# A linear-attention and MLP-mixer kernel: batch 0's u made transposed in PSUM, tokens kept in even and odd halves, other weight pieces, a new order

## The chip, the cores and the metric

The kernel runs on one core of one Trainium2 chip. The time is the device time of one execution in microseconds (us). A core has TensorE (PE; its weight loads are listed apart as PEld), VectorE (DVE), ScalarE (ACT), GpSimd (POOL) and SyncE (SP), and 16 DMA engines that move data between the memory (DRAM) and the on-chip memory (SBUF). PE writes its products to PSUM, which has eight banks of 512 float32 per partition; DVE and ACT read PSUM and write SBUF. SP only issues transfers here, and ACT issues some of the stores.

## The reference

Inputs q, k, v and alpha are (4 batches, 8 heads, 768 tokens, 48 columns), float32. For each batch and head a 48 x 48 state is carried over the tokens:

```
state = alpha[t][:, None] * state + outer(k[t], v[t])
y[t]  = q[t] @ state
```

y, with the heads side by side, is x: (4, 768, 384). A mixer follows, for each batch:

```
h   = relu(x.T @ w_tok1) @ w_tok2        # over tokens: 768 -> 256 -> 768
u   = x + h.T
out = u + relu(u @ w_ch1) @ w_ch2        # over columns: 384 -> 1536 -> 384
```

The output is (4, 768, 384), float32.

## The kernel before, in words

**Attention.** The 768 tokens of a batch are cut into three pieces of 256, so there are twelve pieces n = 0 to 11 (three to a batch). A partition holds two neighbouring tokens ("slots" 0 and 1, even and odd), and one load of 393,216 B brings one of alpha, k, q or v for a piece: `ld_at`, `ld_kt`, `ld_qt`, `ld_vt`. Each piece makes cumulated logarithms of alpha on PE (`cum`), their exponentials (`E`, `IE`), the scaled keys and queries (`kk` and `qq`, tiles pkk and pkq), their transposes, the products of keys and queries (`G`), a causal mask on DVE (`mask`, 1024 columns), the state (`K`, `sa`, `sm`) and two tiles of y that are copied out of PSUM as x (`x0`, `x1`). In pieces 0 to 5 the transposes go over PE (`trk`, `trq`) and an eviction (`evk`, `evq`); in 6 to 11 they are DMA transposes issued by SP (`dk`, `dq`), and the query's is copied once more (`pq`). The eviction of queries (`qev`) writes the two slots of a token pair beside each other, so it writes with a step of two; that of keys (`trwev`) writes runs of 64. Token order inside a tile of 128 rows is therefore the plain one.

**Mixer.** For each batch: t1 (twelve products of 384 columns, from x and w_tok1 into two banks), `ht` (relu to SBUF), t2 (for each of six token tiles two products of 384 columns, out of w_tok2 and ht), `u` (DVE adds x to the bank: tile u, tokens on partitions). c1 needs u transposed (tile ut). In batch 0 (`UP = (0,)`) that is done by PE: `up_0_0` to `up_0_2`, six transposes of 128 x 128 each, and three evictions `ut_0_p`. In batches 1 to 3 it is a DMA transpose on SP for each half of the tokens (`ux`). c1 has twelve column groups mc and two token halves, three products of 384 columns each, and a relu to tile rt on ACT or DVE. c2 sums twelve products for each of six token tiles (in four parts of three), and DVE adds u (`o`, three buffers); the store `st` sends the tile of 128 x 384 to DRAM, from SP's or ACT's queue. The last batch's tile 0 goes in two halves of 192 columns.

**Weights.** Each of 16 weight pieces is loaded by one transfer of 393,216 B and cast to bf16 by ACT, POOL or DVE (`cw`): w_tok1 in two pieces, w_tok2 in two (128 rows each), w_ch1 in six (128 rows by 768 columns), w_ch2 in six (256 rows). c1 of the groups mc below 6 needs w_ch1's pieces 0, 1 and 2, the others need 3, 4 and 5.

**Order.** The program is written out ahead: `ORDER` is a list of operations with a letter for the engine (t PE, s ACT, v DVE, g POOL, y SP), `BUFS` gives each tile its buffer. Every engine goes through its own operations in this order, and waits on semaphores for what it reads and for the buffers that it writes. There are 19 buffers for loads (`in`), four for u, two for ut, three for o, and eight PSUM banks. Entries such as `f8_cumw1` are fillers: products out of a zero tile (line 541 writes it, line 643 multiplies with it) that keep PE running while it waits; the number counts units of 512 columns.

Where a helper does the work, the profile names the helper's line: 643 is `mm` (the products of the attention, and the fillers), 712 the PE transposes of keys and queries, 878 t1, 883 t2, 887 the add of u, 894 the transposes of u, 902 c1, 907 c2, 911 the add of o, 745 and 746 copies and casts on ACT and on the other engines, 770 the mask, 584 loads, 600 to 607 weight loads, 624 the stores, 725 and 729 DMA transposes.

Of the kernel before, what the change touches and what calls it, by code (L numbers as in the profile page):

```python
# [101 lines left out]
UP = (0,)  # L102
# [18 lines left out]
def build(g):  # L121
# [8 lines left out]
    def fillers():  # L130
        for o in list(P.ops):
            nm = o.name
            if "PE" in o.eng and (nm[:4] in ("t1_0", "t2_0", "up_0") or nm.split("_")[-1][-1] in "0123" and nm[:2] not in ("t1", "t2", "up", "c1", "c2") and not nm.endswith("10") and not nm.endswith("11")):
                bank = V("one")
                for z in (1, 2, 3, 4, 6, 8, 12):
                    P.op(f"f{z}_{nm}", {"PE": pe([512] * z)["PE"]}, -100, writes=[bank],
                         emit=lambda e, z=z, bank=bank: g.fill(bank, z))


    def attention(n):  # L140
# [68 lines left out]
        else:  # L209
# [4 lines left out]
                    emit=lambda e: g.trwev(e, tpk, bk, n not in SLOT))  # L214
        if n in QX:
            tqx = V("tpk")
            xq = O("dq", {"SP": (1240.0, 1240.0)}, 9, writes=[tqx], reads=[pkq], preds=qq,
                   emit=lambda e: g.xbar(tqx, pkq), dma=("x", 1400.0, 1180.0, 480.0))
            evq = O("pq", either(dve(1024), act(1024 * 1.35, True), {"POOL": (1100.0, 1140.0)}), 9.5, port=True, writes=[tpq], reads=[tqx], preds=[xq],
                    emit=lambda e: g.qev(e, tpq, g.t(tqx)))  # L220
        else:
            bq = V("one")
            trq = O("trq", pe([128] * 8), 8, writes=[bq], reads=[pkq], preds=qq,
                    emit=lambda e: g.trw(bq, pkq))
            evq = O("evq", either(dve(1024 * 1.065), act(1024 * 1.34)), 9, writes=[tpq], reads=[bq], preds=[trq],
                    emit=lambda e: g.qev(e, tpq, g.bank(bq).bitcast(BF16)))
# [82 lines left out]
    def weight(nm, piece, prio, work=1100.0):  # L309
        raw = V("in")  # L310
        o = P.op(f"ldw_{nm}{piece}", LOADQ[0], prio, writes=[raw],
                 emit=lambda e: g.weight(e, nm, piece, raw, o), dma=("i", work, 1500.0, 650.0))
        wl[(nm, piece)] = P.op(f"cw_{nm}{piece}", either(dve(768, nm != "wc1"), pool_cp(768), act(768, True)), prio + 1,
                               reads=[raw], preds=[o], port=True, emit=lambda e: g.wcast(e, nm, piece, raw))

    def mixer(b):
# [15 lines left out]
        us = []  # L332
        for i in range(NS):
            if i % 3 == 0:
                u = V("u")
            bank = V("one")
            o = P.op(f"t2_{b}_{i}", pe([384] * 2), m0 + (1900 + 330 * i) * sc, writes=[bank],
                     reads=[h for h, _ in hts], preds=[h for _, h in hts] + [wl[("wt2", p)] for p in range(2)],
                     emit=lambda e, i=i, bank=bank: g.tok2(bank, i, [h for h, _ in hts]))
            uo = P.op(f"u_{b}_{i}", dve(384), m0 + (1950 + 330 * i) * sc, writes=[u], reads=[bank, x[i][0]], preds=[o],  # L340
                      emit=lambda e, i=i, bank=bank, u=u: g.uadd(u, i, bank, x[i][0]))
            us.append((u, uo))
        ut = V("ut")
        uts = []
        if b in UP:
            for p in range(3):
                bank = V("one")
                o = P.op(f"up_{b}_{p}", pe([128] * 6), m0 + (3900 + 340 * p) * sc, writes=[bank],
                         reads=list(dict.fromkeys([us[2 * p][0], us[2 * p + 1][0]])),
                         preds=[us[2 * p][1], us[2 * p + 1][1]],  # L350
                         emit=lambda e, p=p, bank=bank: g.utr(bank, [us[2 * p][0], us[2 * p + 1][0]], p))
                uts.append(P.op(f"ut_{b}_{p}", either(dve(768, True), act(768)), m0 + (3950 + 340 * p) * sc, writes=[ut],
                                reads=[bank], preds=[o], emit=lambda e, p=p, bank=bank: g.utev(e, ut, bank, p)))
        else:
            for half in range(2):
                uts.append(P.op(f"ux_{b}_{half}", {"SP": (1240.0, 1240.0)}, m0 + (3900 + 500 * half) * sc, writes=[ut],
                                reads=[us[3 * half][0]], preds=[us[3 * half + i][1] for i in range(3)],
                                emit=lambda e, half=half: g.uxbar(ut, us[3 * half][0], half),
                                dma=("x", 1450.0, 1180.0, 480.0)))
        rts = []  # L360
        for mc in range(NDC):
            rt = V("rt")
            ro = []
            for half in range(2):
                bank = V("one")
                o = P.op(f"c1_{b}_{mc}_{half}", pe([384] * 3), m0 + (4900 + 975 * mc + 487 * half) * sc, writes=[bank],
                         reads=[ut], preds=(uts[0:2 + half] if b in UP else [uts[half]]) + [wl[("wc1", p)] for p in ((0, 1, 2) if mc < 6 else (3, 4, 5))],
# [5 lines left out]
        for i in range(NS):  # L373
            hold = 4000.0 if (i >= NS - 3 and b < B - 1) else 0.0
            cuts = [(0, HD // 2), (HD // 2, HD)] if (b, i) == LAST else [(0, HD)]
            for ci, (ca, cz) in enumerate(cuts):
# [3 lines left out]
                for q4 in range(4):  # L380
                    pp = []
                    for mc in range(3 * q4, 3 * q4 + 3):
# [6 lines left out]
                          reads=[bank, us[i][0]], preds=[prev],  # L389
# [20 lines left out]
ld_at1y ld_at0y ln1s ln0s f8_cumw1t f1_cumw1t cumw1t IE1s cumw0t IE0s ld_vt0y E0s vb0g vs0_0g vs1_0v ld_kt0y kk0v  # L410
f8_trk0t f1_trk0t trk0t E1s ld_qt0y qq0v ka0s kb0s kc0v f1_trq0t trq0t ld_kt1y kk1v K0t evq0s s0_0v ld_vt1y vb1s
f1_trk1t trk1t ld_at2y evk0v ln2s f2_G0_0t G0_0t ld_qt1y ka1g sa1_0v f4_cumw2t cumw2t mask0_0v vs0_1s kb1g kc1g vs1_1s
K1t sm1_0g qq1v sa0_1v sm0_1v G1_0t ld_kt2y IE2s E2s trq1t evq1s ib0t mask1_0v f3_y1_0t y1_0t y0_0t evk1v G0_1t sa1_1v
ld_qt2y x1_0s mask0_1v G1_1t ld_vt2y x0_0s vb2s kk2g trk2t kc2s ldw_wt10y qq2g cw_wt10s f2_ia1t ia1t mask1_1v evk2s
trq2t ld_at3y vs1_2g ldw_wt11y evq2v ib1t y1_1t y0_1t vs0_2g ldw_wt21y sm1_1g P3g K2t sa0_2v sm0_2g x0_1s t1_0_0_0t
f1_G0_2t G0_2t ldw_wt20y G1_2t cw_wt20g t1_0_1_0t mask0_2v x1_1s t1_0_1_1t ld_at4y ld_kt3y t1_0_1_2t lnP3s cum3t
cw_wt11s IE3s ia2t y0_2t x0_2s t1_0_0_1t t1_0_0_2t E3s t1_0_0_3t mask1_2v t1_0_1_3t ib2t y1_2t ldw_wc14y t1_0_1_4t
x1_2s t1_0_0_4t f1_t1_0_1_5t t1_0_1_5t ht_0_1v P4g cw_wt21s t1_0_0_5t ht_0_0s f3_t2_0_0t t2_0_0t t2_0_1t u_0_0v ln13s
r13s ldw_wc13y t2_0_2t u_0_1v t2_0_3t u_0_2v t2_0_5t lnP4s t2_0_4t u_0_3v u_0_5v u_0_4v up_0_0t cw_wc14s cw_wc13s
ldw_wc15y up_0_1t ld_qt3y k0a3g kk3g cum4t trk3t cw_wc15g ut_0_0v up_0_2t ut_0_2v ut_0_1s c1_0_11_0t c1_0_8_0t IE4s  # L420
c1_0_11_1t rt_0_8_0v rt_0_11_0v ldw_wc11y q0r3g qq3g c1_0_9_1t rt_0_9_1v ln14s kb3s c1_0_10_0t cw_wc11s c1_0_9_0t
rt_0_9_0v rt_0_11_1v E4s c1_0_7_0t c1_0_10_1t c1_0_7_1t ldw_wc10y r14s cw_wc10s rt_0_10_1v trq3t evk3s rt_0_7_0v
ldw_wc12y ld_vt3y cw_wc12g c1_0_2_0t c1_0_0_1t ka3g rt_0_7_1s c1_0_8_1t rt_0_10_0v vb3v vs1_3g vs0_3g rt_0_0_1v
rt_0_2_0v evq3s ld_at5y ld_qt4y c1_0_1_1t rt_0_8_1v c1_0_3_0t kc3s K3t P5g c1_0_4_1t rt_0_3_0s rt_0_1_1s q0r4g G0_3t
ld_kt4y qq4g s0_3v ln15s G1_3t sa1_3v c1_0_2_1t rt_0_2_1s mask0_3v lnP5s c1_0_1_0t c1_0_5_1t rt_0_5_1s rt_0_1_0s r15s
mask1_3v ldw_wc21y cw_wc21s k0a4g ldw_wc20y c1_0_6_1t rt_0_6_1v c1_0_4_0t kk4v ldw_wc22y c1_0_5_0t c1_0_0_0t cw_wc22s
rt_0_4_0v rt_0_0_0v cw_wc20g rt_0_4_1s c1_0_6_0t rt_0_6_0v c1_0_3_1t trq4t rt_0_3_1v cum5t trk4t ld_kt5y k0a5g
ldw_wc23y rt_0_5_0s c2_0_3_0t c2_0_5_0t evq4s kb4s evk4v ld_qt5y G1_4t mask1_4v G0_4t ld_vt4y c2_0_0_0t IE5s c2_0_0_1t
ka4g cw_wc23s c2_0_3_1t kc4s sm1_3g E5s mask0_4v ib3t y1_3t ldw_wc24y cw_wc24s c2_0_5_1t vb4g vs1_4s x1_3s ia4t
ldw_wc25y vs0_4g cw_wc25s ld_at6y y0_3t kk5v c2_0_3_2t y0_4t q0r5v trk5t evk5s qq5v K4t c2_0_0_2t sa0_4v c2_0_0_3t P6v  # L430
x0_3s ld_at7y sm0_4g o_0_0v trq5t x0_4s sa1_4v P7g evq5s lnP6s c2_0_5_2t c2_0_5_3t ld_vt5y vb5g c2_0_4_0t c2_0_4_1t
ld_kt7y kc5g G1_5t G0_5t lnP7s o_0_5v ib4t y1_4t vs1_5s mask1_5v t1_1_1_0t t1_1_1_1t sm1_4g x1_4s c2_0_4_2t c2_0_3_3t
vs0_5s ld_at8y t1_1_1_2t st_0_5s K5t mask0_5v sa0_5v sm0_5v cum6t t1_1_0_0t ld_kt6y k0a6g t1_1_0_1t ld_qt6y c2_0_2_0t
# [532 lines left out]
```

## Time and profile before

| | |
|---|---|
| median of three runs | 163.48 us (163.34, 163.48, 164.39) |
| span of the profiled execution | 160.5 us |
| PE busy | 154.6 us, 1563 products |
| DVE, ACT, POOL busy | 114.9, 97.8, 80.8 us |
| DMA | 35.05 MB in 76130 packets, mean 218 GB/s |

The three runs are executions of their own; the profiled execution is known by its span, the time from its first to its last instruction, and the median of the runs is 3.0 us longer than that. Times within the profile count from the span's start. PE's busy time is that of pipelined products whose ends are modelled, so a mean of one product (326 ns at 384 columns) is longer than its share of the stream. A share of the DMA engines is the time that packets took, over sixteen engines; packets can overlap.

### The profile page before, as it was taken

Reading aid. Unit: us, or ns where it says so; the run is one execution under the profiler, and the core shown is the slowest. Engines: PE = TensorE matmul, PEld = TensorE weight load, DVE = VectorE, ACT = ScalarE, POOL = GpSimd, SP = SyncE. Lnnn points to the kernel's source line nnn. Section 1 sums busy time; section 2 is a strip of 40 time slices with the busy share of each in tenths; the row PEclk is TensorE's granted clock in tenths of the full one; section 3 lists DMA queues with packets and bytes.
Section 4 is the critical chain, followed back from the end, with each engine's and each line's share of the span. In section 5 each row is a group of like instructions: output and inputs, shape, how many; then the busy total and the mean of one; then the engine's idle time right before and its main releaser. Section 6 shows DMA issues by size and latency. Waiting matters only on the chain.

```text
span 160.5 us, 3971 instructions
## 1 busy us (share of the span) xinstructions
PE 154.6 (96%) x1563; PEld 97.1 (60%) x1563; DVE 114.9 (72%) x206; ACT 97.8 (61%) x179; POOL 80.8 (50%) x94
## 2 busy tenths in 40 slices
PE   7999989999999999999999999999999999999992
PEld 2545565766667676666667666566567665665661
DVE  6099994979889787989969758795886762464222
ACT  3789999998899955897563583269832203343000
POOL 5205897695973649389778852699523000000000
PEclk9999999999999999999999999999999999999999
DMA  4999999999999999999989999989701235111133
GB/s 122 320 324 317 317 374 311 339 333 306 316 347 324 275 278 272 210 228 319 241 202 298 239 315 204 217 196 134 196 21 62 87 79 169 49 49 53 49 129 116
DMA packets 76130, 35.05 MB, mean 218 GB/s; under 512 B 70352, under 2 KB 74320, under 8 KB 76112
## 3 DMA queue, kind: packets, MB, share of 16 engines
q1 hardware_dynamic: 73808, 31.76, 74.1%
q10 hardware_dynamic: 2304, 3.05, 5.3%
q8 instruction: 12, 0.20, 0.5%
q14 instruction: 6, 0.05, 0.1%
HBM read 25.17 MB, written 4.72 MB: 186 GB/s over the span
## 4 chain that ended last, share of the span: by engine, by line
PE 61%; DMA 12%; DVE 6%; ACT 6%; SPq 6%; POOL 4%; issue 3%; DVEq 0%; POOLq 0%
PE ps L907 22%; PE ps L902 21%; PE ps L643 11%; DMA in<-in_v_dram 6%; SPq L584 6%; DMA out_dram<-o 4%; PE ps L878 3%; PE ps L883 2%; DMA ut<-u 2%; DVE pkk L700 2%; DVE gtm L770 1%; PE ps L712 1%; DVE rt L875 1%; POOL vb L746 1%; POOL pkq L700 1%
## 5 line engine op out<-in xcount | busy, mean ns | idle before, releaser
L907 PE MATMUL ps<-wc,rt 128*128 128x384 bf16 (+1 forms) x300 | 52.4, 319 | 0.0
L902 PE MATMUL ps<-ut,wc 128*128 128x384 bf16 x288 | 50.3, 326 | 0.1
L902 PEld LDWEIGHTS <-wc 128*128 128x128 bf16 x288 | 27.1, 98 | 17.9 <-DMA ut<-u 0.6
L907 PEld LDWEIGHTS <-rt 128*128 128x128 bf16 x300 | 27.8, 98 | 16.0
L873 ACT ACTIVATE rt<-ps 128x384 bf16<-128x384 f32 x47 | 21.4, 492 | 23.6 <-PE ps L902 23.3
L875 DVE TENSOR_SCALAR rt<-ps 128x384 bf16<-128x384 f32 x49 | 25.6, 551 | 9.1 <-PE ps L902 8.9
L770 DVE TENSOR_TENSOR gtm<-ps,mk 128x1024 bf16<-128x1024 f32 x24 | 28.5, 1218 | 3.1 <-PE ps L643 2.8
L911 DVE TENSOR_TENSOR o<-ps,u 128x384 f32<-128x384 f32 (+1 forms) x25 | 13.2, 536 | 12.6 <-PE ps L907 10.1
L700 POOL TENSOR_TENSOR pkk<-in,IE 128x768 bf16<-128x768 f32 x8 | 14.5, 1817 | 3.3 <-DVE ss L844 2.3
L745 ACT CAST x<-ps 128x384 bf16<-128x384 f32 x20 | 9.2, 479 | 11.1 <-PE ps L643 9.5
L887 DVE TENSOR_TENSOR u<-ps,x 128x384 bf16<-128x384 f32 x24 | 12.0, 550 | 3.1 <-PE ps L883 2.5
L746 POOL CAST vb<-in 64x384 bf16<-64x384 f32 (+1 forms) x14 | 8.3, 594 | 10.4 <-DMA in<-in_v_dram 4.7
L692 POOL TENSOR_TENSOR in<-in,in 128x384 f32<-128x384 f32 x8 | 8.0, 1000 | 10.5 <-DVE u L887 3.8
L643 PE MATMUL ps<-rt 128*128 128x512 bf16 (+1 forms) x29 | 12.1, 515 | 1.1 <-DVE rt L541 1.1
L745 ACT CAST vb<-in 64x384 bf16<-64x384 f32 (+1 forms) x18 | 11.4, 634 | 0.8 <-DMA in<-in_v_dram 0.3
L700 POOL TENSOR_TENSOR pkq<-in,E 128x768 bf16<-128x768 f32 x6 | 10.9, 1818 | 0.6 <-DMA tpk<-pkq 0.3
L878 PE MATMUL ps<-x,wt 128*128 128x384 bf16 x48 | 11.0, 325 | 0.0
L844 POOL TENSOR_TENSOR ss<-tmp,E 128x384 bf16<-128x384 f32 x10 | 8.3, 833 | 4.2 <-DVE in L628 3.9
L841 DVE TENSOR_TENSOR tmp<-ps,ss 128x384 f32<-128x384 f32 x16 | 8.8, 552 | 1.8 <-PE ps L643 0.6
L883 PE MATMUL ps<-ht,wt 128*128 128x384 bf16 x48 | 9.1, 326 | 0.0
L643 PE MATMUL ps<-vb,gtm 128*128 128x48 bf16 x192 | 8.2, 183 | 0.2 <-DVE gtm L770 0.2
L643 PE MATMUL ps<-tpq,tpk 48*64 48x128 bf16 (+1 forms) x288 | 7.9, 218 | 0.4 <-POOL tpq L746 0.3
(94 smaller groups left out, 207.6 us busy)
## 6 DMA issues: line engine op xcount, KB each, us to landing
in<-in_alpha_dram SPq DMA_DIRECT2D x12, 384.0 KB, 5.1
in<-in_v_dram SPq DMA_DIRECT2D x12, 384.0 KB, 5.6
in<-in_k_dram SPq DMA_DIRECT2D x12, 384.0 KB, 5.2
in<-in_q_dram SPq DMA_DIRECT2D x12, 384.0 KB, 5.5
in<-in_moe_w_ch_dram SPq DMA_DIRECT2D x12, 384.0 KB, 5.9
out_dram<-o ACTq DMA_DIRECT2D x15, 192.0 KB, 1.8
in<-in_moe_w_tok_dram SPq DMA_DIRECT2D x4, 384.0 KB, 6.0
out_dram<-o SPq DMA_DIRECT2D x8, 192.0 KB, 2.2
```

Of the source, the lines that this page charges most:

```text
L643: return self.pe.matmul(out, lhsT=lhsT, rhs=rhs, start=start, stop=stop, skip_group_check=True)
L700: self.shared(self.eng[e].tensor_tensor(self.t(dst)[:, :, h0:h1, 0:D], self.t(src)[:, h0:h1].rearrange("p h s d -> p s h d"), bass.AP(tens ...
L745: return self.act.copy(d, s)
L770: self.nc.vector.tensor_tensor(self.t(gtm)[:, hf, :, :], self.pair(gp).rearrange("p a (j t) -> p (a j) t", t=128), bass.AP(tensor=m.tensor ...
L873: self.act.activation(d, s, AF.Relu)
L875: self.nc.vector.tensor_scalar_max(d, s, 0.0)
L878: self.pe.matmul(self.bank(bank)[:, 0:HD], lhsT=self.wt1[:, kc, m * 128 : m * 128 + 128], rhs=self.t(x), start=(kc == 0), stop=(kc == NS - 1))
L883: self.pe.matmul(self.bank(bank)[:, 0:HD], lhsT=self.wt2[:, kc, i * 128 : i * 128 + 128], rhs=self.t(hts[kc]), start=(kc == 0), stop=(kc = ...
L887: self.nc.vector.tensor_tensor(self.t(u)[:, i % 3], self.bank(bank)[:, 0:HD], self.t(x), ALU.add)
L902: self.pe.matmul(self.bank(bank)[:, 0:HD], lhsT=self.wc1[:, kc, mc * 128 : mc * 128 + 128], rhs=self.t(ut)[:, 3 * half : 3 * half + 3, kc, ...
L907: self.pe.matmul(self.bank(bank)[:, 0 : cz - ca], lhsT=self.t(rts[mc][0])[:, i * 128 : i * 128 + 128], rhs=self.wc2[:, mc, ca:cz], start=( ...
L911: self.nc.vector.tensor_tensor(self.t(o)[:, ca:cz], self.bank(bank)[:, 0 : cz - ca], self.t(u)[:, i % 3, ca:cz], ALU.add)
```

## The change

**Batch 0's u.** `UP` becomes empty and `UDIR = (0,)` is new. For batch 0 and each token half, three banks (one for each 128 columns j) first take x transposed: `xadd` multiplies three tiles of x with the identity, 128 columns each, into one bank (`xa_0_half_j`, 18 products in all). Then `tok2t` adds the t2 products with the operands exchanged, ht as the stationary one and w_tok2 as the moving one (`tt_0_half_j`, two products of 384 columns), so that the bank holds u transposed. `utev3` evicts it to ut (`ut_0_half_j`, on ACT four times and on DVE twice). The adds u_0_i and the PE transposes up_0_p fall away. Because the o adds need u with tokens on partitions, `unat` transposes ut back by a DMA transpose on SP for each half (`un_0_0`, `un_0_1`).

**Token order.** Inside each tile of 128 rows, the even tokens now come first and the odd ones after them. `qev` and `trwev` become one function, `merged`, that writes runs of 64. The masks are built for this order (tiles of the same size). w_tok1's rows are loaded in that order, each piece by two transfers to 64 partitions, and w_tok2's columns are put in that order by its cast. The store sends row (s, p) of a tile to row 2p + s of out.

**Weight pieces.** w_tok2 is cut by columns (one piece to a token half), w_ch1 by columns (256 to a piece, all 384 rows), so that c1 of group mc needs piece mc // 2 alone, and a token half of t2 one piece of w_tok2.

**Order.** ORDER and BUFS are new throughout. The opening now loads alpha of piece 0 first. Its fillers are f12 and f4 ahead of `cumw0`, f6 ahead of `trk0`, f2 ahead of `K0`, f3 ahead of `G0_0` and f2 ahead of `trk2`: 29 units, where there were 36.

```diff
-UP = (0,)
+UP = ()
+UDIR = (0,)
...
-                    emit=lambda e: g.qev(e, tpq, g.bank(bq).bitcast(BF16)))
+                    emit=lambda e: g.merged(e, tpq, g.bank(bq).bitcast(BF16)))
...
+        if b in UDIR:
+            ut, us, uts = V("ut"), [], []
+            for half in range(2):
+                evs = []
+                for j in range(NM):
+                    bank = V("one")
+                    tx = x[3 * half : 3 * half + 3]
+                    xa = P.op(f"xa_{b}_{half}_{j}", pe([128] * 3), ...
+                    o = P.op(f"tt_{b}_{half}_{j}", pe([384] * 2), ...
+                              preds=[h for _, h in hts] + [xa, wl[("wt2", half)]], ...
+                    evs.append(P.op(f"ut_{b}_{half}_{j}", either(act(384), dve(384)), ...
+                uts.append(evs)
+                u = V("u")
+                un = P.op(f"un_{b}_{half}", {"SP": (1240.0, 1240.0)}, ... reads=[ut], preds=evs, ...
+                us += [(u, un)] * 3
...
-  preds=(uts[0:2 + half] if b in UP else [uts[half]]) + [wl[("wc1", p)] for p in ((0, 1, 2) if mc < 6 else (3, 4, 5))],
+  preds=(uts[half] if b in UDIR else uts[0:2 + half] if b in UP else [uts[half]]) + [wl[("wc1", mc // 2)]],
...
+            w = self.w[0].rearrange("(c p s) m -> s p c m", p=64, s=2)[part]
+            self.gated(dma(t[64 * part : 64 * part + 64].rearrange("p (c m) -> p c m", c=3), w[:, 3 * piece : 3 * piece + 3, :]), op)
...
+            w = self.w[2].rearrange("(c p) m -> p c m", p=128)
+            self.gated(dma(t.rearrange("p (c m) -> p c m", c=3), w[:, :, 256 * piece : 256 * piece + 256]), op)
...
+    def rows(self, d):
+        return d.rearrange("(p s) c -> s p c", s=2)
+
     def store(self, e, o, b, i, ca, cz):
-        self.queue(e).dma_start(self.out[b, i * 128 : (i + 1) * 128, ca:cz], self.t(o)[:, ca:cz])
+        self.queue(e).dma_start(self.rows(self.out[b, i * 128 : (i + 1) * 128, ca:cz]), self.t(o)[:, ca:cz])
...
+    def merged(self, e, d, s):
+        self.copy(e, self.t(d).rearrange("p (g s t) -> p s g t", g=8, s=2), s.rearrange("p (s g t) -> p s g t", s=2, g=8))
...
+    def xadd(self, bank, xs, j):
+        for i, x in enumerate(xs):
+            self.mm(self.bank(bank)[:, i * 128 : i * 128 + 128], self.t(x)[:, j * 128 : j * 128 + 128], self.idn, i == 0, False)
+
+    def tok2t(self, bank, half, j, hts):
+        for kc in range(NDT):
+            self.mm(self.bank(bank)[:, 0:HD], self.t(hts[kc])[:, j * 128 : j * 128 + 128],
+                    self.wt2[:, half, kc, :], False, kc == NDT - 1)
+
+    def utev3(self, e, ut, bank, half, j):
+        self.copy(e, self.t(ut)[:, 3 * half : 3 * half + 3, j, :], self.bank(bank)[:, 0:HD].rearrange("p (i t) -> p i t", i=3))
+
+    def unat(self, u, ut, half):
+        self.nc.sync.dma_start_transpose(self.t(u).rearrange("p i (j c) -> p (i j) c", j=NM),
+                                         self.t(ut)[:, 3 * half : 3 * half + 3].rearrange("p i j t -> p (i j t)"))
```

Of the new ORDER, the stretch around batch 0's mixer, and the end:

```
... x1_2s t1_0_0_4t t1_0_1_5t ht_0_1v ldw_wt21y t1_0_0_5t IE3s kk3g ht_0_0s xa_0_1_1t xa_0_0_2t xa_0_1_0t xa_0_1_2t cw_wt21s
tt_0_0_1t ut_0_0_1s tt_0_0_0t ut_0_0_0s tt_0_0_2t ut_0_0_2v ldw_wc13y cw_wc13g tt_0_1_2t ut_0_1_2s tt_0_1_1t ut_0_1_1v tt_0_1_0t
ut_0_1_0s ka3s trk3t evk3v c1_0_7_0t rt_0_7_0v ldw_wc14y cw_wc14g c1_0_9_0t ...
... o_3_1v st_3_1s rt_3_6_1s st_3_0h1s c2_3_5_0t c2_3_2_2t c2_3_2_3t rt_3_4_1v c2_3_5_1t rt_3_9_1s c2_3_5_2t c2_3_5_3t o_3_5v o_3_2v
st_3_2y st_2_0y st_3_5s c2_3_3_0t c2_3_4_0t c2_3_4_1t c2_3_4_2t c2_3_4_3t o_3_4v st_3_4s c2_3_3_1t c2_3_3_2t c2_3_3_3t o_3_3v
st_3_3y c2_3_0h0_2t c2_3_0h0_3t o_3_0h0v st_3_0h0s
```

More of the change, by code (lines that the diff above doesn't have):

```diff
@@ L310, in weight @@
         raw = V("in")
-        o = P.op(f"ldw_{nm}{piece}", LOADQ[0], prio, writes=[raw],
-                 emit=lambda e: g.weight(e, nm, piece, raw, o), dma=("i", work, 1500.0, 650.0))
+        ls = {}
+        for z in range(2 if nm == "wt1" else 1):
+            ls[z] = P.op(f"ldw_{nm}{piece}{'ab'[z] if nm == 'wt1' else ''}", LOADQ[0], prio, writes=[raw],
+                         emit=lambda e, z=z: g.weight(e, nm, piece, z, raw, ls[z]),
+                         dma=("i", work / (2 if nm == "wt1" else 1), 1500.0, 650.0))
         wl[(nm, piece)] = P.op(f"cw_{nm}{piece}", either(dve(768, nm != "wc1"), pool_cp(768), act(768, True)), prio + 1,
-                               reads=[raw], preds=[o], port=True, emit=lambda e: g.wcast(e, nm, piece, raw))
+                               reads=[raw], preds=list(ls.values()), port=True, emit=lambda e: g.wcast(e, nm, piece, raw))
     def mixer(b):
```

277 lines of the change are left out of this document (135 added, 142 removed), and 22 rows, old and new, of the table BUFS.

## The prediction

> **What bounds the kernel now.** I read the page first, then the busy time of each engine by stretches, then the timelines of the opening and of the end.
>
> ```profile
> span 160.5 us, 3971 instructions
> ...
> PE 154.6 (96%) x1563; PEld 97.1 (60%) x1563; DVE 114.9 (72%) x206; ACT 97.8 (61%) x179; POOL 80.8 (50%) x94
> ...
> q1 hardware_dynamic: 73808, 31.76, 74.1%
> q10 hardware_dynamic: 2304, 3.05, 5.3%
> ...
> L643 PE MATMUL ps<-rt 128*128 128x512 bf16 (+1 forms) x29 | 12.1, 515 | 1.1 <-DVE rt L541 1.1
> ```
>
> PE is busy for 154.6 of 160.5 us, and 12.1 us of that are fillers (L643 out of a zero tile), all in the first 28 us. So PE does about 142.5 us of work, and what can be gained lies ahead of the first channel product (c1, L902); from there PE runs almost without a gap, and anything that stops it costs its whole length. The other number to keep is the DMA's: 74% of sixteen engines on SP's queue. In stretches:
>
> ```profile
> 2.00:28.00 26.00, 24.75 (x274) 13.43 (x273) 19.16 (x36) 21.64 (x34) 14.47 (x21) 1.00 1.10 320
> ...
> 70.00:81.00 11.00, 11.00 (x120) 6.96 (x119) 10.35 (x19) 7.44 (x15) 9.21 (x7) 1.00 1.10 256
> 81.00:94.00 13.00, 13.00 (x190) 8.73 (x188) 9.79 (x15) 7.47 (x17) 11.13 (x12) 1.00 0.96 254
> ...
> 114.00:129.00 15.00, 14.72 (x168) 9.80 (x166) 11.59 (x19) 5.16 (x10) 3.80 (x6) 1.00 0.28 84
> 129.00:133.00 4.00, 4.00 (x27) 2.38 (x25) 2.44 (x6) 0.00 (x0) 0.00 (x0) 1.00 0.52 118
> ...
> 137.00:144.00 7.00, 7.00 (x45) 4.21 (x43) 4.16 (x8) 2.94 (x7) 0.00 (x0) 1.00 0.15 56
> ```
>
> The columns are the stretch, busy time (and count) of PE, PEld, DVE, ACT and POOL, the granted clock, the mean busy share of the 16 DMA engines, and GB/s. The share reads 1.10 while loads arrive (packets of one engine overlap), and stays near 1 up to 94 us: the DMA engines have little to spare until then, and it is hidden only because loads run ahead.
>
> **The opening.** The change makes batch 0's u transposed at once. These rows stand between the last x and c1 now:
>
> ```profile
> 21.30 1.30 DVE L746 COPY tpq<-ps 128x1024 bf16<-128x1024 bf16 x1
> ...
> 27.73 2.28 PE L883 MATMUL ps<-ht,wt 128*128 128x384 bf16 x12
> 29.85 0.83 PE L894 MATMUL ps<-idn,u 128*128 128x128 bf16 x12
> 30.52 0.33 PE L643 MATMUL ps<-la,u 128*128 128x384 bf16 x1
> ...
> 30.81 0.61 PE L712 MATMUL ps<-idn,pkk 128*128 128x128 bf16 x8
> 31.25 0.50 PE L894 MATMUL ps<-idn,u 128*128 128x128 bf16 x6
> 31.76 4.55 PE L902 MATMUL ps<-ut,wc 128*128 128x384 bf16 x27
> ...
> 30.16 0.88 POOL L746 CAST wc<-in 128x768 bf16<-128x768 f32 x1 [0.36 <-DMA in<-in_moe_w_ch_dram]
> ...
> L873 ACT ACTIVATE ht<-ps 128x384 bf16<-128x384 f32 x4 | 1.9, 489 | 2.2 <-PE ps L878 2.2
> ...
> L887 DVE TENSOR_TENSOR u<-ps,x 128x384 bf16<-128x384 f32 x24 | 12.0, 550 | 3.1 <-PE ps L883 2.5 <-issue 0.4
> ...
> L746 DVE COPY tpk<-ps 128x1024 bf16<-128x1024 bf16 x3 | 2.0, 679 | 0.0
> ...
> 133.97 10.72 PE ps L902 x66
> ```
>
> (Timeline rows are start, length; the ht, u and tpk rows are groups, with total and mean in ns; the last is a piece of the chain that ended last.) A 384-column product takes 10.72/66 = 0.162 us of the stream. From the start of t2 to c1 it is 31.76 - 27.73 = 4.03 us: twelve products (1.95), six adds on DVE, 18 transposes, their evictions. After, the twelve products go into banks that already hold x, six evictions follow them closely (four on ACT, two on DVE), and PE does only trk3 (0.44, from 30.81 to 31.25 now) before c1: 1.95 + 0.45 = 2.4, saved 1.6. The 18 products with the identity that add x are as many and as large as the 18 transposes removed, and stand in waits ahead of ht; six adds of 0.55 us leave DVE, four evictions of 0.49 come to ACT, beside PE. The last query eviction goes from a strided write, 1.30, to runs of 64, for which I take the key eviction's 0.68: 0.6 less on the last x. cum4 (30.52 to 30.81, 0.3) now comes behind c1 and is still to be done. Together -1.6 - 0.6 + 0.3 = **-1.9 us**. The weights no longer bind: c1 needed three pieces of w_ch1, the last cast at 30.16 to 31.04, the 22nd load; now it needs one, the 19th, and a load takes 393,216 B / 320 GB/s = 1.23 us, so 3.7 us earlier. Bounds of this term: 0 (the new order waits as long elsewhere) and -3.7 (all that the loads allow). If ACT, at 21.64 of 26 us, runs late with the four evictions, c1 slips by up to 0.5 each. Seven filler units fewer (36 to 29, 0.2 us each) change nothing while they only fill waits. The two new DMA transposes (u back to its plain order) are on SP's queue, ahead of loads of batch 2 and needed only by the o adds; they cost DMA time, counted below. The masks, whose shape doesn't change, are free, as are the setup copies.
>
> **The stores.** This is the part that decides. With tokens in halves, row p of a tile is no longer row p of out; `store` now names the DRAM side as (half, pair, column), 2 x 64 x 384, where it was 128 x 384. The bytes and runs (1,536 B) are the same, so counted by packets it costs nothing. The question is how the rows are dealt to the DMA engines.
>
> ```profile
> L624 ACTq DMA_DIRECT2D out_dram<-o x16: 338/338/390, 56.9 to 157.0; - x16
> L624 SPq DMA_DIRECT2D out_dram<-o x9: 332/530/2601, 66.0 to 157.8; - x9
> ...
> DMA to landing us min/median/max: 1.6/2.0/5.8
> ```
>
> q10 carries ACT's 16 stores alone: 2304 / 16 = 144 packets each, 128 rows and 16 more, one for each engine: a store's outermost count, 128, is dealt in sixteen equal shares. Every load and store of before has 128 outermost on both sides, so no row shows what a 2 gives. Two bounds: sixteen engines as now, or two, half a tile each. The nearest row in form is the present store, but what it shows is a deal by equal shares of the outermost count, which 2 cannot give to sixteen; I take two engines.
>
> [...]
>
> Price of a store: from 137 to 144 us there are two stores and nothing else on the DMA (56 GB/s x 7 us = 2 x 196,608 B): 0.15 x 7 x 16 / 2 = 8.4 us of engine time each; by q10, 0.053 x 160.5 x 16 / 15.5 = 8.8. Over sixteen engines that is 0.53 us, over two **4.3 us**. PE makes one such tile in 12 x 0.162 = 1.95 us when it does nothing else, and there are three o tiles, so DVE's o add waits for the store three back. That wait exists already in small (0.39 and 1.64 us):
>
> ```profile
> 53.51 0.55 DVE L911 TENSOR_TENSOR o<-ps,u 128x384 f32<-128x384 f32 x1
> ...
> 70.02 0.56 DVE L911 TENSOR_TENSOR o<-ps,u 128x384 f32<-128x384 f32 x1 [0.39 <-DMA out_dram<-o]
> 87.04 0.55 DVE L911 TENSOR_TENSOR o<-ps,u 128x384 f32<-128x384 f32 x1
> ...
> 134.74 0.56 DVE L911 TENSOR_TENSOR o<-ps,u 128x384 f32<-128x384 f32 x1 [1.64 <-DMA out_dram<-o]
> ...
> 157.44 0.36 DVE L911 TENSOR_TENSOR o<-ps,u 128x192 f32<-128x192 f32 x1 [0.43 <-PE ps L907]
> ...
> 57.47 1.77 SPq L584 DMA_DIRECT2D in<-in_k_dram  x1
> ...
> 113.31 0.58 SPq L584 DMA_DIRECT2D in<-in_v_dram  x1
> ...
> 129.54 2.90 SPq L729 DMA_TRANSPOSE ut<-u  x2
> ```
>
> Behind a waiting o add on DVE stand the u adds, masks and half of the relus, and PE needs all of them. Every load and transpose also has a share on the two engines and lands only when these are done; a store on SP's queue holds the transposes and loads behind it.
>
> So I count the work of the two busiest engines from the first store (56.9) on. Stores: 24 whole tiles x 4.3 = 103. Loads: 17 (57.47 to 113.31) x 1.23 = 21. Transposes: in 129 to 133, 0.52 x 4 x 16 = 33.3, less one store of 8.4, is 12.4 us for each of the two, 0.78 per engine; 18 now and 2 new, 16. Sum 140 us, where they have 160.5 - 57 = 103. Two corrections: where packets of several transfers overlap, 1.10 us of packet time went into 1 us, so 140 / 1.10 = 127; and between the o adds of two batches (70.02 to 87.04, 17 us) three waiting tiles drain in 13, so I leave 4 us idle after batch 0 and after batch 1. Span: 57 - 1.9 + 127 + 8 + 1.1 (landing 1.6 less its 0.5 of packets) = 191. The median of the runs, 163.48, is 3.0 over the profiled span, so **194 us**. Ends of this sum: tail alone (below) about 178; no overlap, idle as estimated, and issues that block ACT (SP's longest store issue is 2.6 us) 215.
>
> **Rivals.**
> (1) Two engines, but only the end pays: middle stores find room because loads run ahead. For it: batch 0's o adds are spread over 16.5 us (53.51 to 70.02), and the DMA share is 0.28 from 114 to 129 us. Against it: share near 1 until 94 us, and 140 us of work in 103. At the end there is no room: after o_3_1 the new order has 42 whole and 6 half products, 7.3 us, and seven tiles' worth of stores (one left over from batch 2), 7 x 4.3 = 30. PE's work ends at 157.4 now (the last o add): 157.4 - 1.9 - 7.3 + 30 + 1.1 + 3 = 182; with the overlap 179. About **181 us**.
> (2) Sixteen engines carry the new stores, so that the change does only what it says in the opening: 163.5 - 1.9 = **161.6 us**. It decides the sign: it holds if the rows are dealt out by the SBUF side's 128 alone, and no row here excludes that.
> (3) Sixteen engines, but the new order loses elsewhere: a load or a transpose that comes late in the middle stops PE. The waits of before show one such stop, short, on the copy of a transposed query:
>
> ```profile
> PE ps L643 <- POOL tpq L746: 0.3, 1, 0.3
> ```
>
> Three or four stops of 1 us, each as long as a transpose holds SP's queue (2.90 us for two), give 163 to 167, **165 us**.
>
> **How the numbers follow.** Forecast 0.60 (its own range 184 to 215), rival 1 0.17, rival 2 0.15, rival 3 0.08. Predicted time 194. Leaving out rivals 2 and 3 would leave out 0.23 and a bit above 215, so the range reaches down to 161. A measurement tells 1% (1.6 us). Slower: 0.60 + 0.17 + half of rival 3, 0.81; within 1%: 0.04; faster: 0.15.
>
> **What would show it.** Two engines: packets per store on ACT's queue fall from 144 to 130, issue to landing goes from 2.0 us to 5 and more, DVE's idle time ahead of L911's line is released by the DMA of out for tens of us, PE falls far below 96%, and the end has some 20 us of stores after the last product. The opening: first c1 at about 29.4 us. Wrong: a landing of about 2 us for stores and a span near 159; or landings of 5 us with PE still above 90% up to the last c2, which is rival 1.

## The result, and the profile after

| | median | ratio to before | span of the profiled execution |
|---|---|---|---|
| before, same chip | 163.41 us (4 runs) | 1 | 160.5 us |
| changed kernel | 234.81 us (4 runs, 233.85 to 236.22) | 1.437 (1.428 to 1.446) | 232.1 us |

The change makes the kernel 71.4 us slower. The forecast was 194 us, at most 215: the direction was right, and so was the deal of a store over two engines, but the loss was 2.3 times the 31 us foreseen.

The page of the changed kernel, the lines that answer to those of before (the row PEclk is the granted clock in forty slices of the span, DMA the share of sixteen engines):

```profile
span 232.1 us, 3966 instructions
PE 163.4 (70%) x1555; PEld 100.2 (43%) x1555; DVE 116.4 (50%) x209; ACT 98.0 (42%) x187; POOL 67.0 (29%) x80
...
PE   8888999999981099997297487807998799910000
PEclk9999999999997559999769979986999999995555
DMA  7999999999999999997496976993018110101111
...
q1 hardware_dynamic: 78134, 32.84, 70.0%
q10 hardware_dynamic: 1820, 2.56, 3.2%
...
L943 DVE TENSOR_TENSOR o<-ps,u 128x384 f32<-128x384 f32 (+1 forms) x25 | 12.9, 537 | 54.2 <-DMA out_dram<-o 47.0
L934 PE MATMUL ps<-ut,wc 128*128 128x384 bf16 x288 | 55.1, 345 | 19.8 <-DMA ut<-u 13.2
```

PE went from 96% to 70%. q10, ACT's queue, carries 14 stores (two of them half as wide): 1820 / 14 = 130 packets each, 128 rows and two more, where there were 144. The packets beyond the rows are of 4 B: 28 for these 14 stores, 256 for the 16 of before. DVE's o add (L943) stands 47 us behind the DMA of out. The long holes in PE's row begin after 64 us (the first store is issued at 61.7), and in some of them, and at the end, PE is granted about half its clock.

The stretches (PE, PEld, DVE, ACT, POOL, clock, DMA share, GB/s):

```profile
70.00:76.00 6.00, 0.53 (x7) 0.27 (x5) 0.83 (x2) 1.52 (x3) 3.08 (x3) 0.71 1.97 140
...
81.00:88.00 7.00, 6.66 (x27) 3.42 (x28) 2.68 (x6) 1.22 (x4) 0.00 (x0) 0.63 1.06 237
...
160.00:175.00 15.00, 15.00 (x179) 9.82 (x178) 11.33 (x19) 3.33 (x8) 1.67 (x2) 0.96 0.08 25
190.00:205.00 15.00, 13.86 (x97) 8.77 (x95) 1.94 (x4) 2.00 (x5) 0.00 (x0) 1.00 0.07 23
...
220.00:232.00 12.00, 0.00 (x0) 0.00 (x0) 0.36 (x1) 0.00 (x0) 0.00 (x0) 0.50 0.12 44
```

The last row is the mechanism in the open: only stores are left, and the share is 0.12 of sixteen engines, which is two (2 / 16 = 0.125): by the packet records exactly two packets are open for 8.7 of the 11 us from 221 to 232. They move 44 GB/s, so a whole tile of 196,608 B takes 4.5 us; the forecast had 4.3. From 190 to 205 the share is 0.07: the two stand idle almost half the time while PE works, and later PE is done and they are not. From 70 to 76 it is the other way round: PE stands, the share is 1.97, and yet only 140 GB/s move. The packet records of the trace show where that share comes from: 2080 packets begin in these 6 us, and 18 of them, all of 256 B, stay open for 1 us and more and hold 75 of the 189 us of packet time. Without these 18 the share would be 1.19, near the 1.14 that the same 6 us have with plain stores (the first experiment below). Packets of 256 B are the transposes': the count of them, 21,504, falls by 2304 in the run below that leaves two transposes out.

Pieces of the chain that ended last (start, length, what it waited for or did), and of the timeline:

```profile
70.38 10.92 DMA ut<-u
81.34 3.07 PE ps L934 x9
...
143.97 13.95 DMA tpk<-pkk
...
207.46 13.76 DMA out_dram<-o
```

```profile
81.34 12.27 PE L934 MATMUL ps<-ut,wc 128*128 128x384 bf16 x60 [9.48 <-DMA ut<-u]
...
194.84 9.02 PE L939 MATMUL ps<-wc,rt 128*128 128x384 bf16 x57
...
221.34 0.36 DVE L943 TENSOR_TENSOR o<-ps,u 128x192 f32<-128x192 f32 x1 [2.89 <-DMA out_dram<-o]
```

A transpose of u lands 10.9 us after its issue began, and one of the keys 13.95 us after. PE stands 9.48 us for the first and then runs c1 slowly (nine products in 3.07 us, 0.34 each, against 0.162 at full clock). The last product ends at 194.84 + 9.02 = 203.9 us; the 28 us after it go to stores.

### The profile page after: what moved, and what is told of

The parts are those of the page before. It is cut to its first block, busy times and chain, and to the rows that moved or that the text cites. A ratio compares the mean times of both kernels' runs of the same rounds, so it can differ in the third digit from the quotient of the medians.

```text
span 232.1 us, 3966 instructions
## 1 busy us (share of the span) xinstructions
PE 163.4 (70%) x1555; PEld 100.2 (43%) x1555; DVE 116.4 (50%) x209; ACT 98.0 (42%) x187; POOL 67.0 (29%) x80
## 3 DMA queue, kind: packets, MB, share of 16 engines
q1 hardware_dynamic: 78134, 32.84, 70.0%
q10 hardware_dynamic: 1820, 2.56, 3.2%
## 4 chain that ended last, share of the span: by engine, by line
DMA 52%; PE 21%; SPq 9%; DVE 4%; ACT 3%; POOL 2%; issue 2%; ACTq 0%; DVEq 0%; POOLq 0%
DMA out_dram<-o 23%; DMA in<-in_alpha_dram 8%; DMA tpk<-pkk 8%; PE ps L939 8%; PE ps L934 6%; DMA tpk<-pkq 5%; DMA ut<-u 5%; SPq L604 5%; PE ps L667 3%; PE ps L894 3%; DMA in<-in_moe_w_ch_dram 3%; SPq L620 2%; DVE o L943 2%; PE ps L899 2%; SPq L623 1%
## 5 line engine op out<-in xcount | busy, mean ns | idle before, releaser
L934 PE MATMUL ps<-ut,wc 128*128 128x384 bf16 x288 | 55.1, 345 | 19.8 <-DMA ut<-u 13.2
L939 PE MATMUL ps<-wc,rt 128*128 128x384 bf16 (+1 forms) x300 | 55.4, 325 | 0.5 <-DVE x L763 0.3
L889 ACT ACTIVATE rt<-ps 128x384 bf16<-128x384 f32 x58 | 26.2, 492 | 42.0 <-PE ps L934 33.7
L943 DVE TENSOR_TENSOR o<-ps,u 128x384 f32<-128x384 f32 (+1 forms) x25 | 12.9, 537 | 54.2 <-DMA out_dram<-o 47.0
L891 DVE TENSOR_SCALAR rt<-ps 128x384 bf16<-128x384 f32 x38 | 19.8, 552 | 12.9 <-PE ps L934 12.8
L724 POOL TENSOR_TENSOR pkk<-in,IE 128x768 bf16<-128x768 f32 x6 | 10.9, 1816 | 5.3 <-DVE pkq L724 4.5
L667 PEld LDWEIGHTS <-tpk 48*64 48x64 bf16 (+1 forms) x288 | 6.5, 109 | 12.6 <-DMA tpk<-pkk 8.0
L652 POOL TENSOR_TENSOR in<-in 128x384 f32<-128x384 f32 x9 | 9.0, 1003 | 8.9 <-DMA in<-in_alpha_dram 8.8
L763 POOL COPY kt<-pkk 64x384 bf16<-64x384 bf16 x9 | 4.5, 503 | 24.1 <-DVE tpq L763 10.8
L903 DVE TENSOR_TENSOR u<-ps,x 128x384 bf16<-128x384 f32 x18 | 8.8, 550 | 4.0 <-PE ps L899 4.0
L667 PE MATMUL ps<-rt 128*64 128x384 f32 (+1 forms) x21 | 8.9, 552 | 1.0 <-DVE rt L566 1.0
```

Source lines behind the costliest of these rows:

```text
L667: return self.pe.matmul(out, lhsT=lhsT, rhs=rhs, start=start, stop=stop, skip_group_check=True)
L724: self.shared(self.eng[e].tensor_tensor(self.t(dst)[:, :, h0:h1, 0:D], self.t(src)[:, h0:h1].rearrange("p h s d -> p s h d"), bass.AP(tens ...
L763: return self.shared(self.eng[e].tensor_copy(d, s))
L889: self.act.activation(d, s, AF.Relu)
L891: self.nc.vector.tensor_scalar_max(d, s, 0.0)
L934: self.pe.matmul(self.bank(bank)[:, 0:HD], lhsT=self.wc1[:, kc, mc * 128 : mc * 128 + 128], rhs=self.t(ut)[:, 3 * half : 3 * half + 3, kc, ...
```

## The experiments

Theory D (the deal): what costs is that a store whose DRAM side has an outermost count of 2 runs on two DMA engines. Its rivals were the rest of the change (new order, `un`, weight pieces), the end alone, and, once D stood, the way in which the stores cost: through the o adds that wait for them, or through the engines that loads and transposes share with them. All diffs are against the changed kernel, except where another is named.

**The changed kernel with plain stores.** The rows of out come in another order.

```diff
-        self.queue(e).dma_start(self.rows(self.out[b, i * 128 : (i + 1) * 128, ca:cz]), self.t(o)[:, ca:cz])
+        self.queue(e).dma_start(self.out[b, i * 128 : (i + 1) * 128, ca:cz], self.t(o)[:, ca:cz])
```

> The changed kernel with the store's DRAM side plain again (128 x 384 instead of 2 x 64 x 384), so rows of out come in another order; all else as changed. Theory A (the stores on two engines are all of the 71 us): 160.5 to 162.5 us, 144 packets a store again, which would also measure the opening's gain (1.9 us forecast). Rival B (the new order, its two more transposes and the new weight pieces lose a good part on their own): over 166 us.

168.16 us, ratio 1.035 (1.033 to 1.037), span 167.0. One line takes 66.6 us away, but the range of theory A is missed: rival B holds for the rest. Its page, its stretches and its last products:

```profile
PE 153.9 (92%) x1555; PEld 97.2 (58%) x1555; DVE 116.2 (70%) x209; ACT 97.1 (58%) x187; POOL 66.8 (40%) x80
...
q1 hardware_dynamic: 78288, 32.84, 78.1%
q10 hardware_dynamic: 2016, 2.56, 5.3%
```

```profile
0.00:28.00 28.00, 24.61 (x286) 15.08 (x287) 20.39 (x51) 20.23 (x33) 15.32 (x23) 1.00 1.06 287
28.00:50.00 22.00, 21.59 (x196) 13.44 (x195) 17.56 (x29) 20.11 (x41) 13.20 (x16) 1.00 1.04 321
50.00:70.00 20.00, 17.79 (x199) 11.86 (x196) 14.33 (x25) 11.71 (x22) 10.33 (x12) 1.00 1.14 255
70.00:114.00 44.00, 40.03 (x411) 24.97 (x408) 35.15 (x60) 27.80 (x57) 17.89 (x20) 1.00 1.08 245
114.00:167.00 53.00, 49.89 (x473) 31.88 (x470) 28.74 (x49) 17.25 (x38) 10.05 (x11) 1.00 0.32 88
```

```profile
154.94 8.95 PE L939 MATMUL ps<-wc,rt 128*128 128x384 bf16 x57
```

2016 / 14 is 144 packets again, and the clock is full throughout. What is left of the change costs 168.16 - 162.43 (before, beside it) = 5.7 us.

**Before, with the stores of the changed kernel alone.**

```diff
+        d = self.out[b, i * 128 : (i + 1) * 128, ca:cz].rearrange("(p s) c -> s p c", s=2)
+        self.queue(e).dma_start(d, self.t(o)[:, ca:cz])
```

> The kernel before with nothing changed but the store's DRAM side, 2 x 64 x 384 as in the changed kernel (rows of out come in another order). Theory A: 220 to 240 us, 130 packets a store. Rival B: under 200 us.

228.65 us, ratio 1.409 (1.403 to 1.415): +66.2 us, by the store alone, in the old order. 66.2 and 5.7 add up to 71.9, and the whole change costs 71.4 (its runs spread over 2.4 us). D is shown from both sides.

```profile
q10 hardware_dynamic: 2080, 3.05, 4.1%
...
DVE o L912 <- DMA out_dram<-o: 42.3, 12, 7.8
```

(2080 / 16 = 130 packets. A row of waits is: who waits for what, us in total, times, the longest.)

**Outermost 8 and outermost 4.** Same bytes and runs, s = 8 and then s = 4 instead of 2; the rows go elsewhere in the tile.

```diff
-        return d.rearrange("(p s) c -> s p c", s=2)
+        return d.rearrange("(p s) c -> s p c", s=8)
```

> The changed kernel with the store's DRAM side 8 x 16 x 384 (rows of out in another order): the same runs and bytes with an outermost count of 8. If rows are dealt in equal shares of the outermost count: eight engines, 136 packets a store, 1.1 to 1.2 us on each, 161 to 165 us. Rival (stores whose rows are apart in DRAM are slow whatever the outermost count): over 200 us.

> The changed kernel with the store's DRAM side 4 x 32 x 384 (rows of out in another order): four engines, 132 packets a store, 2.1 us on each. Theory C (the prediction's sum of work on the busiest engines, which counts only when it exceeds the time there is): 24 x 2.1 + 21 + 16 = 87 us in 103, so the middle is hidden and the end costs 6 x 2.1 - 7.3 = 5 us: 173 to 178 us. Theory L (every transpose and o add waits for the slowest engine's share of a store, so the loss goes with a store's time on an engine, 1/k less 1/16): 66.6 x 0.1875 / 0.4375 = 28.5, so 190 to 200 us.

Outermost 8: 175.4 us, ratio 1.078 (1.075 to 1.081). Outermost 4: 197.49 us, ratio 1.213 (1.205 to 1.220). ACT's queue and its issues, first for 8, then for 4 (the last row's numbers are the shortest, median and longest issue in ns):

```profile
q10 hardware_dynamic: 1904, 2.56, 4.7%
...
L648 ACTq DMA_DIRECT2D out_dram<-o x14: 614/614/1210, 60.2 to 170.9; - x14
```

```profile
q10 hardware_dynamic: 1848, 2.56, 4.1%
...
L648 ACTq DMA_DIRECT2D out_dram<-o x14: 547/547/1141, 60.1 to 187.4; - x14
```

136 and 132 packets: counted as the 144 and 130 above, 128 and one for each engine, so eight and four engines. A tile's 8.4 us of engine time (0.15 x 7 x 16 / 2, before, from 137 to 144 us) would take 8.4 / k on k engines, an estimate (4.2 for two, where 4.5 were measured); that is 3.7, 1.6 and 0.53 us more than on sixteen for k = 2, 4 and 8. Over the kernel with plain stores they cost 66.6, 29.3 and 7.2 us: about 18, 19 and 14 times the extra of one store, of 24 tiles. Outermost 8 was expected at 161 to 165 us and missed that by 10; outermost 4 came out in theory L's range, not in theory C's. By C's count the four engines have 87 us of work in 103 (24 x 2.1 for stores, 21 for loads, 16 for transposes), and only the end should cost. So the sum of the work from the first store to the last doesn't give the time. Two things are not shown by this. The engines may still lack capacity for a while: from 57 to 94 us the DMA share is 1.12 with plain stores already. And 18 or 19 is no count of waits: with outermost 4 PE's last product ends at 178.7 us, against 163.9 with plain stores, and 15.4 us of stores follow it, against 3.1. Of the 27 us between the two spans, 15 lie ahead of that product and 12 behind it.

**Only the last batch, and only the first three.**

```diff
+        d = self.out[b, i * 128 : (i + 1) * 128, ca:cz]
+        self.queue(e).dma_start(self.rows(d) if b == B - 1 else d, self.t(o)[:, ca:cz])
```

> The changed kernel, the store's DRAM side 2 x 64 x 384 for batch 3's tiles alone, plain (128 x 384) for batches 0 to 2; rows of out come in another order. This is the tail by itself: after o_3_1 7.3 us of products and six tiles of stores at 4.8 us (196,608 B at the 40 GB/s that two engines moved at the end) are left, against 3 us now: 168.2 + 28.8 + 1.1 - 7.3 - 3.1 = 187 to 189 us. Rival (the queues of the two engines take it in at once, as nothing else moves then): under 180.

> The other half: 2 x 64 x 384 for batches 0 to 2, plain for batch 3. If the middle pays (two engines are the bound from 61 us on): what is left of the 66.6 us, 168.2 + 47 = 205 to 218 us. If only the end pays: under 175 us.

The last batch alone: 191.97 us, ratio 1.180 (1.172 to 1.188), 23.8 above plain stores and 3 above the range expected. The first three (the condition is `b < B - 1`): 211.92 us, ratio 1.299 (1.289 to 1.309), 43.8 above. This is the range in which the middle pays. The two add up to 67.6, where both together cost 66.6, so the losses are separate, and the middle is the larger one. What SP's queue took of sixteen engines, last batch alone and then the first three:

```profile
q1 hardware_dynamic: 78260, 32.84, 68.6%
```

```profile
q1 hardware_dynamic: 78162, 32.84, 78.0%
...
PE ps L935 <- DMA ut<-u: 13.0, 3, 9.6
PE ps L668 <- DMA tpk<-pkk: 8.0, 1, 8.0
```

Times their spans (189.4 and 211.0 us) this is 130 and 165 us of sixteen engines, against 0.781 x 167.0 = 130 with plain stores and 0.700 x 232.1 = 162 in the changed kernel, for the same 32.84 MB. At the end the two engines work alone and nothing else is touched. In the middle the packets of SP's queue are open for 32 to 34 us more, as a mean over sixteen engines, with no byte more to move. In the changed kernel 28 of its 32 us more are in the transposes' packets of 256 B, and 23 are in packets that stay open for over 1 us (206 of 78134, against 64 with plain stores). The median packet of a transpose takes 18 ns and that of a load of 384 B takes 22 ns in both kernels. So it is the transposes beside the stores that wait, each through a few packets.

**Stores that no o add waits for.** Each store reads a constant tile of weights, so an o tile is free as soon as the add has written it; the sums don't reach out.

```diff
+        src = self.wc2[:, 0:2, :].rearrange("p c m -> p (c m)").bitcast(F32)
+        self.queue(e).dma_start(self.rows(self.out[b, i * 128 : (i + 1) * 128, ca:cz]), src[:, ca:cz])
```

> The changed kernel, but the stores send a part of the w_ch2 tile instead of o: the same transfers on the same two engines, and no o add has to wait for a store (out holds weights). Theory W (the o adds' waits on DVE, 47 us, carry the loss): PE's last product comes by 175 us and the end is set by the queue of stores alone, 61 + 24 x 4.8 = 176 and up: 178 to 195 us. Theory S (loads and transposes are late because each has a share on the two engines): 210 to 232 us, with PE waiting on ut, tpk and tpq.

219.8 us (216.78 to 221.79), in theory S's range. The 47 us that DVE stands behind stores carry only 234.8 - 219.8 = 15 us of the 66.6, give or take the 5 us over which these runs spread. Even of these, most are at the end: PE's last product comes 4.5 us earlier than in the changed kernel (199.4 us, not 203.9; 163.9 with plain stores). PE's longest waits stay where they were, a line further down in this kernel:

```profile
PE ps L935 <- DMA ut<-u: 12.7, 2, 8.2
PE ps L668 <- DMA tpk<-pkk: 7.0, 1, 7.0
```

```profile
190.44 8.95 PE L940 MATMUL ps<-wc,rt 128*128 128x384 bf16 x57
```

The row with the largest idle time was not the largest cause. The rest of the middle's loss, by elimination, is transfers that come late beside the stores. Whether they wait at the two engines or behind stores in SP's own queue wasn't separated; a run with all stores on ACT's queue would tell.

**Plain stores without the two transposes back.** `unat` issues nothing, and the u of batch 0 that the o adds read is a tile of zeros.

```diff
-        self.nc.sync.dma_start_transpose(...)
+        pass
```

> The changed kernel with plain stores and without the two DMA transposes that turn batch 0's u back (its u is zero in the o adds; rows of out in another order). If the two transposes, which held SP's queue for 4.5 and 3.5 us at 49 and 62 us, are what the rest of the change loses after 50 us: 161 to 163.5 us. If the new order loses it elsewhere: 166 to 168 us.

166.74 us, ratio 1.027 (1.021 to 1.033): 1.4 us less than with them (1.033 to 1.037, so the two intervals just meet), and in the range in which the new order loses elsewhere. In stretches:

```profile
50.00:70.00 20.00, 20.00 (x216) 13.36 (x215) 17.32 (x30) 14.31 (x28) 10.99 (x13) 1.00 0.96 263
70.00:114.00 44.00, 40.12 (x409) 25.20 (x408) 34.62 (x58) 28.03 (x58) 18.19 (x23) 1.00 1.06 242
```

PE's idle 2.2 us between 50 and 70 are gone; the 3.9 between 70 and 114 have another cause.

**Two ways to split a store.** In the first, each slot goes by a transfer of its own, from 64 partitions to 64 rows of out, so that every row lands where the reference has it. In the second, a control, each plain store goes as two transfers of 128 rows by half the columns.

```diff
+        d = self.rows(self.out[b, i * 128 : (i + 1) * 128, ca:cz])
+        for s in range(2):
+            self.queue(e).dma_start(d[s], self.t(o)[64 * s : 64 * s + 64, ca:cz])
```

```diff
+        m = (ca + cz) // 2
+        for c, z in ((ca, m), (m, cz)):
+            self.queue(e).dma_start(self.out[b, i * 128 : (i + 1) * 128, c:z], self.t(o)[:, c:z])
```

> The changed kernel with each store as two transfers of 64 partitions, one for each token half, every one with 64 rows outermost on both sides; the output is the reference's. Theory A: sixteen engines again, as the plain store or up to 1 us more for 25 more issues of 0.34 us: 160.5 to 163.5 us. Rival B: over 166 us.

> The changed kernel with each store plain in DRAM but as two transfers of 128 x 192 (rows of out in another order). The version with two transfers of 64 partitions took 175.0 us, 6.8 more than one plain transfer. If the second issue (0.6 us each on ACT and SP, where one plain store takes 0.34) is the cost: 172 to 176 us. If it is the 64 partitions or the rows apart in DRAM: 168 to 170 us.

The halves: 174.99 us, ratio 1.080 (1.076 to 1.084), 6.8 above plain stores, so rival B. The columns: 173.04 us, ratio 1.060 (1.053 to 1.068), 4.9 above, in the range given to the second issue. ACT's queue and issues, halves and then columns:

```profile
q10 hardware_dynamic: 2240, 2.56, 5.2%
...
L650 ACTq DMA_DIRECT2D out_dram<-o x28: 473/608/1167, 61.4 to 171.1; - x28
```

```profile
q10 hardware_dynamic: 4032, 2.56, 4.6%
...
L650 ACTq DMA_DIRECT2D out_dram<-o x28: 338/442/1533, 61.1 to 169.4; - x28
```

2240 / 28 = 80 packets, 64 and sixteen: all engines are back, and 60 of the 66.6 us with them. What the remaining 6.8 us are is open. The columns pay 4.9 us for a second issue too, but they differ in a second way: 4032 / 28 = 144 packets a transfer, so twice the packets of a plain store at half the size, where the halves have 160 packets a store. The second issue alone was not tested.

No kernel here beat the one before.

## Why the prediction was right or wrong

**The deal over the engines: right**, and so is its price per tile. 130 packets, 0.12 of sixteen engines at the end, 4.5 us per tile against 4.3 forecast. Rival 2 (sixteen engines, 161.6 us) falls with 234.8 us and with the 66.2 us that the store alone costs in the old order. Two engines was my estimate, and so was that they are the same two for every store, on which the sum of their work rests: the kernel before has no store with an outermost count other than 128 (144 packets), so its trace shows neither. The packet counts for outermost 2, 4 and 8 (130, 132, 136) and the two packets open at the end of the changed kernel agree with the first. For the second there is that end too: 16 packets of SP's stores begin every 0.49 us while they are alone (214.5 to 220.3 us) and every 0.98 us beside one of ACT's (222.4 to 226.3), as they would on two engines that both queues share.

**The end: nearly right.** 23.8 us by the last batch alone; by rival 1 it was 181 - 161.6 = 19 (17 with the overlap). With the first three batches in it, the forecast's loss from stores was 194 - 161.6 = 32 us, so it left 12 to 15 for the middle. Measured: 43.8. Rival 1 (only the end pays) falls with that.

**The step that failed: the sum of the work on the two busiest engines.** It added up 140 us, divided by an overlap of 1.10 and allowed 8 us idle, as if the two engines would work without a break from the first store to the last. That is a lower bound, and I took it for the time. Three rows show what it left out. First, the two engines don't run through: 0.08 and 0.07 of sixteen engines from 160 to 175 and from 190 to 205 us are 1.3 and 1.1 engines of two, so each of the two is idle for some 12 us in these 30 alone, where I had left 8 us for the whole kernel. Second, PE's work passes over the DMA engines many times (loads, transposes of keys and of u, o tiles), and transfers there come late in turn: a transpose of u lands after 10.9 us (median 3.6, longest 4.7 with plain stores), one of the keys after 13.95 (median 4.4, longest 6.0). Outermost 4 shows the same failure: by the sum only its end would cost, and 15 us are lost ahead of PE's last product. That PE pays such a wait at each passage is argued, not counted. Third, PE was slower after its stops (nine products of c1 in 3.07 us, 0.34 each, after the one of 9.5 us, against 0.162): PE's busy time is 163.4 us against 153.9 with plain stores for the same 1555 products, 9.5 us that no sum of transfers holds. By the clock records PE was busy for 16.4 us while it was granted half its clock, which is worth some 8 of them (an estimate: half of 16.4). The rest of the 65.1 us between the two spans, 55.6, is idle.

The upper end had the same fault: it varied the overlap and the issues, and took no case in which waits add up along the chain.

**Who waits.** I named DVE's o adds first and the shared engines second. The o adds have the larger row (47 us) and the smaller cause (15 us).

**The opening: the direction right, the amount not.** The start of t2 with its operands exchanged, and the first c1:

```profile
27.61 2.12 PE L667 MATMUL ps<-wt,ht 128*128 128x384 bf16 x12
...
30.12 0.66 PE L934 MATMUL ps<-ut,wc 128*128 128x384 bf16 x3
```

This is in the kernel with plain stores. From t2 to c1 it is 2.5 us; 2.4 were forecast, and it was 4.03. But t2 starts at 27.61, hardly earlier than the 27.73 of before: the 0.6 us of the query eviction don't reach it, though the eviction itself is as taken (0.69 us in the changed kernel, forecast 0.68). Why not was not tried. So c1 comes at 30.12, 1.6 us earlier than the 31.76 of before; the forecast was 29.4. In the changed kernel t2 starts at 28.23 and c1 at 30.73, 1.0 us earlier.

What counts is the work left. Without fillers both kernels have the same 1534 products. Counted at 0.162 us for 384 columns, the kernel with plain stores has 1.2 us less of them to do than before at 40 us and 0.5 us less at 50 us; the forecast was 1.9. The changed kernel is level with before at 40 us and 1.2 us behind at 50.

PE's busy time would mislead here. Before:

```profile
0.00:28.00 28.00, 25.70 (x275) 13.94 (x276) 19.95 (x45) 22.84 (x34) 15.72 (x29) 1.00 1.02 298
28.00:50.00 22.00, 21.92 (x215) 14.38 (x214) 19.15 (x33) 20.19 (x36) 17.03 (x18) 1.00 1.04 330
50.00:70.00 20.00, 19.97 (x213) 13.28 (x212) 16.73 (x29) 15.61 (x31) 11.02 (x12) 1.00 1.03 268
70.00:114.00 44.00, 43.93 (x515) 27.95 (x514) 35.28 (x59) 27.62 (x58) 33.22 (x31) 1.00 0.99 229
114.00:161.00 47.00, 43.12 (x353) 27.50 (x350) 23.74 (x42) 11.59 (x24) 3.80 (x6) 1.00 0.27 86
```

Up to 50 us PE was busy for 25.70 + 21.92 us, of it 12.3 in fillers, which leaves 35.3; in the kernel with plain stores it is 24.61 + 21.59 less 8.9, 37.3. That looks like 2.0 us more work done. But after 50 us PE is busy for 107.7 us there and for 107.0 before: a single product of 384 columns counts 0.32 us there, one in a stream 0.162, so busy time is no measure of work.

**The rest of the order: wrong, rival 3 was true of it.** The lead of 0.5 us at 50 us turns into a loss of 5.7 with plain stores. Between 50 and 114 us PE is idle 6.2 us there (0.1 before). I had costed the two transposes back at their DMA time alone, because only the o adds need them. They also hold SP's queue:

```profile
48.89 4.47 SPq L929 DMA_TRANSPOSE u<-ut  x1
...
61.84 3.54 SPq L929 DMA_TRANSPOSE u<-ut  x1
```

4.47 and 3.54 us while the DMA share is above 1, with loads queued behind; taking them out gives 1.4 us back (their DMA time and an o add's wait for them, 1.5 us, go with them, so the hold alone is not priced). The other 3.9 us of idle time from 70 to 114 are several short waits, for a copy of a query, for an o add, for a transpose of u (0.7 to 1.3 us each without `un`). That is rival 3's picture (stops of about 1 us; 165 us forecast, 168.2 measured), but which part of the new order makes them was not separated, and of the 5.7 us only what the idle time shows is placed.

## What to carry to other kernels

Look at the outermost count of a store's DRAM side before counting bytes: one `rearrange` of it, with the same bytes and runs, cost 41% in the old order (228.65 us), and the packets per store told it in one line of the profile (144, 136, 132 and 130 for 128, 8, 4 and 2 outermost). The sum of the work on the few busiest DMA engines was only a lower bound here: it gave a span of 191 us where 232.1 were measured, with PE waiting on transposes (one of 10.9 us, one of 13.95) and o tiles in turn. The loss was 14 to 19 times the extra time of one store, of 24 tiles; that factor was measured in this kernel and not derived. Compare two orders by the products that are left, not by PE's busy time. And take the largest row of waits for a suspect only; taking that wait away showed 15 us where its row showed 47.

## What the runs showed of the hardware that was not expected

- A DMA share above 1 needn't mean that the engines are full. From 70 to 76 us the share is 1.97 at 140 GB/s, and 18 packets of transposes make the difference to 1.19; over the changed kernel SP's queue has packets open for 162 us of sixteen engines, against 130 with plain stores, for the same bytes. The share is a mean: on which engines the long packets stand is not in the record.
- The time to issue a store depends on its form: a median of 338 ns (plain), 522 (outermost 2), 547 (4) and 614 (8):

```profile
L648 ACTq DMA_DIRECT2D out_dram<-o x14: 522/522/2260, 61.7 to 221.7; - x14
```

- PE's clock followed its long stops: 0.71 in the stretch in which it stops (70 to 76 us), 0.63 in the one in which c1 takes up again (81 to 88), 0.50 at the end (220 to 232) with nothing to multiply. In the changed kernel's clock records, the stop of 9.5 us (71.9 to 81.3) goes with a clock of 0.50 from 72.5 to 86.1 us, that of 4.2 (110.7 to 114.9) with 0.50 from 113.5 to 120.3, that of 7.9 (150.1 to 158.0) with 0.50 from 154.4 to 161.2, and after the last product (203.9) it is 0.50 from 209.0 on. Shorter stops had it too: there one of 2.9 us (131.5 to 134.3) goes with 0.50 from 133.9 to 137.3, and with the stores in halves one of 2.0 us (71.6 to 73.5) is followed by a clock of 0.50 up to 77.1 us (0.84 as a mean from 70 to 81), while in the changed kernel the clock stays at 1.00 over one of 2.6 us (126.2 to 128.9). So the length of one stop alone doesn't decide here. In the kernel with plain stores, whose stops are up to about 1.5 us, the clock stays at 1.00.
